# Gaps in SBUF that put the operands of TensorE at multiples of 512 bytes, in a Fourier transform with a bilinear expert

## The chip, the core and the metric

The kernel runs on one core of one Trainium2 chip. The metric is the device time of one execution in microseconds (us). TensorE (PE) does the matrix products, VectorE (DVE), ScalarE (ACT) and GpSimd (POOL) the elementwise work, and SyncE (SP) and POOL issue the DMAs. SBUF is the memory that holds the engines' operands; a byte address in this text is one within a partition, and every tile has the same address in all of its 128 partitions. PSUM takes TensorE's results.

## The reference

```python
X = np.fft.fft(x, axis=1)             # x: 8 x 3072 x 256, float32
X = np.fft.fft(X, axis=2).real
X = X.reshape(8 * 3072, 256)
a = X @ w_a                           # 256 x 1536
b = X @ w_b                           # 256 x 1536
out = (a * b) @ w_out                 # 1536 x 256
```

## The kernel before

The transform along the 256 features is folded into the weights: `w_a` and `w_b` are multiplied once, at the start, by a cosine and a sine matrix (`WChunk`, L497, plain float32), and the result stands in SBUF in two tiles, `W0` and `W1`. The transform along the 3072 positions is done for each of the 8 batches by matmuls of the folded input with tables of cosines and sines: `dft_mm` (L179) and `dft_quad` (L191), whose moving operand is a table `tab` and whose stationary operand (weights, in TensorE's sense) is `XH`, the folded input. The results are the rows of `PQ`: 1536 frequencies wide, a cosine part and a sine part.

A number is kept as a sum of a high and a low part of type float32r, and each product is made in three passes, high by high, high by low and low by high (`PASSES`). So each table holds a high and a low row for each of three blocks: `tab` is `[P, 3, 2, TW]`, with `TW` numbers of 4 bytes in a row. The first 386 of them at most are read.

The main work is 288 units: 8 batches `b`, 3 blocks `st` of 512 frequencies, 12 blocks `ft` of 128 of the 1536 hidden features. A unit has 24 matmuls with 512 columns each:

- `mm_e` (L759), 6 matmuls: the cosine part of `PQ` is the moving operand, 128 columns of `W0` or `W1` are the weights. The result is `ab`, one PSUM bank for `a` and one for `b`.
- `mm_o` (L773), 6 matmuls: the same with the sine part of `PQ`, added to `ab`.
- `mm_d` (L851), 12 matmuls: the product `a * b` (its high part `gh` and its low part `gl`) is the moving operand, every second column of a row of `WO` (a step of 8 bytes, 128 columns) the weights. The result is `d`, held for the 12 `ft` of a block.

```python
nc.tensor.matmul(ab[i], wcols(lh, 0, i, ft * P, P), PQ[:, rh, st * 512 : (st + 1) * 512], ...)   # L759
nc.tensor.matmul(cur["d"][s][h], WO[:, rh, ft, h:D:2], gg[lh][:, s, :], ...)                     # L851
```

Between them DVE, ACT and POOL turn `ab` into `gh` and `gl`. In the last block of the last batch `mm_rows` (L726) takes `gh` and `gl` as weights and 256 columns of `WO` as the moving operand, and `ExUp` and `ExDown` (L958, L962, L987, L990) do 48 matmuls with very few weight columns for two single frequencies.

The order of the work is written out by hand in the list `units` and by the function that walks through it. Tiles come from pools. A pool's tiles lie behind each other in the order of their first request, each rounded up to 32 bytes, and the pools lie behind each other in the order in which they were made. A pool with two buffers (`tb` for the tables, `t`, `bc`, `g`) repeats its tiles. `PQ` and `PN` are requested late, in the middle of the set-up, and are the last tiles of the pool `per`; `tb` is the pool behind it, and `t`, `bc`, `g` and the staging follow; the pool `late` with `W1` and `XH` is last.

Of the kernel before, what the change touches and what calls it, by code (L numbers as in the profile page):

```python
# [7 lines left out]
F32 = mybir.dt.float32  # L8
# [3 lines left out]
ALU = mybir.AluOpType  # L12
PSUM = bass.MemoryType.PSUM

TW = 386

@with_exitstack
def fft2_real__then__bilinear_moe_kernel(
# [26 lines left out]
    P = 128  # L45
# [4 lines left out]
    J = S // 8  # L50

    per = ctx.enter_context(tc.tile_pool(name="per", bufs=1))
    dram = ctx.enter_context(tc.tile_pool(name="dram", bufs=1, space=bass.MemoryType.DRAM))
    tb_p = ctx.enter_context(tc.tile_pool(name="tb", bufs=2))
    t_p = ctx.enter_context(tc.tile_pool(name="t", bufs=2))
# [3 lines left out]
    ps_ab = ctx.enter_context(tc.tile_pool(name="ps_ab", bufs=2, space=PSUM))  # L59
    ps_d = ctx.enter_context(tc.tile_pool(name="ps_d", bufs=1, space=PSUM))  # L60

    W0 = per.tile([P, 2, 2, 1024], F32R, name="W0")
    WO = per.tile([P, 2, NFT, D], F32R, name="WO")
    w128 = per.tile([P, 2 * NFT], F32, name="w128")
# [20 lines left out]
    def f32(ap):  # L85
        return ap.bitcast(F32)

    def split(lo_eng, hi, lo, src):
        nc.scalar.copy(hi, src)
        lo_eng.tensor_tensor(lo, src, f32(hi), ALU.subtract)  # L90
# [65 lines left out]
    def sign_ops(kind):  # L156
        f = F[:, kind, 0:5:4, :]
        nc.scalar.activation(f, f, AF.Copy, scale=sm[:, 0:1])
        f = F[:, kind, 2, :]
        nc.scalar.activation(f, f, AF.Copy, scale=sm[:, 1:2])  # L160
# [9 lines left out]
    def load_tab(half, q):  # L170
        t = tb_p.tile([P, 3, 2, TW], F32R, tag="tab", name="tab")
        nc.gpsimd.dma_start(t.rearrange("p a b c -> p (a b c)"), tabs[3 * half + q])
        tabq[(half, q)] = t
# [10 lines left out]
    def dft_quad(ps, lhs, r, tab, swap):  # L184

        own, e, o = r
        for rr, kt, c0, c1 in ((own, own // 2, 0, TW), (o, 0, 0, J // 2), (e, 0, J // 2, TW)):
            if kt == 0 and swap:
                rr = e + o - rr
            for k, (lh, rh) in enumerate(PASSES):  # L190
                nc.tensor.matmul(  # L191
                    ps[:, c0:c1], lhs(lh, rr), tab[:, kt, rh, c0:c1],
                    start=(c1 - c0 == TW and k == 0), stop=(c1 == TW and kt == 0 and k == 2), skip_group_check=True,
                )

    def dft_pair4(q, ps=None):
        ps = ps or ab_tiles()

        def lhs(h, r):
            return XH[:, h, q, r, :]  # L200

        dft_quad(ps[0], lhs, (5, 1, 3), tabq[(0, 2 * q)], q == 1)
        dft_quad(ps[1], lhs, (2, 0, 4), tabq[(0, 1)], q == 1)
        return ps
# [20 lines left out]
    def dft_pair32(kind, half, q, ps, f=None):  # L225

        f = f or (lambda r: F[:, kind, r, :])
        for i, (t, n) in enumerate(((q, halves(half)[2] if q == 0 else J), (1, J))):
            for kt in range(3):
                nc.tensor.matmul(  # L230
                    ps[i][:, 0:n], f(2 * kt + 1 - i), tab32[(half, t)][kt][:, 0:n], start=(kt == 0), stop=(kt == 2)
                )
# [15 lines left out]

    def halves(half):
        cols = slice(2 * J * half, 2 * J * (half + 1))  # L250
        return cols, (J + 1 if half == 0 else J), (TW if half == 0 else J)

    def pairs2(v):
        return v.rearrange("p (i t) -> p i t", t=2)
# [1 line left out]
    def combine(dst, a, ps, m, quad=False):  # L256

        lo, hi, av, cv = dst[:, 0:J], dst[:, J : 2 * J][:, ::-1], a[0:m, 0:J], ps[1][0:m, 0:J]
        if quad:
            lo, hi, av, cv = pairs2(lo), pairs2(hi), pairs2(av), natural(ps[1][0:m], J // 2)  # L260
        nc.vector.tensor_tensor(lo, av, cv, ALU.add)
        nc.vector.tensor_tensor(hi, av, cv, ALU.subtract)
# [9 lines left out]
    class DftP:  # L272
# [4 lines left out]
        def mm(self, ps=None):  # L277
            if self.b == 0:
                self.ps = ps
                return dft_pair32(2 * self.half, self.half, 0, ps)  # L280
            if self.quad:
                self.ps = dft_pair4(0, ps)
                return
            self.ps = dft_pair(
                lambda h, kt: XH[:, h, 0, 2 * kt + 1, :], lambda h, kt: XH[:, h, 0, 2 * kt, :],
                self.half, 0, halves(self.half)[2], ps,
            )

        def copy(self):
            b, half, ps = self.b, self.half, self.ps  # L290
            n0 = halves(half)[1]
            a = self.a = bc_p.tile([P, 512], F32, tag="bc", name="bc")
            evened(a, ps[0], n0, self.quad, zb[:, half, b : b + 1])

        def sums(self):
            b, half, ps, a = self.b, self.half, self.ps, self.a
            self.t = t_p.tile([P, 1024], F32, tag="T", name="T")[:, 0 : 2 * J]
            combine(self.t, a, ps, P, self.quad)
            nc.scalar.copy(PQ[:, 0, halves(half)[0]], self.t)

# [5 lines left out]
        def low(self, lo_eng=nc.gpsimd):  # L306
            cols = halves(self.half)[0]
            lo_eng.tensor_tensor(PQ[:, 1, cols], self.t, f32(PQ[:, 0, cols]), ALU.subtract)

# [64 lines left out]
    class DftQ:  # L374
# [53 lines left out]
        def split(self, lo_eng=nc.gpsimd):  # L428
            cols, _, _ = halves(self.half)

            nc.scalar.copy(self.t[0:1, :], PN[0:1, cols])
            split(lo_eng, PQ[:, 2, cols], PQ[:, 3, cols], self.t)

# [49 lines left out]
    def wcols(h, eo, i, c, n):  # L483

        return W0[:, h, eo, 512 * i + c : 512 * i + c + n] if c < 512 else W1[:, h, eo, 1024 * i + c - 512 : 1024 * i + c - 512 + n]

# [33 lines left out]
    class WHalf:  # L520
# [12 lines left out]
        def dst(self, lh, eo):  # L533
            return W0[:, lh, eo, :].rearrange("p (i c) -> p i c", i=2)[:, :, 256 * self.h : 256 * (self.h + 1)]

# [83 lines left out]
    for half in range(2):  # L619
        t = tb_p.tile([P, 3, 2, TW], F32, tag="tab", name="tab32").rearrange("p a b c -> p (a b c)")  # L620
        for q in range(3):
            v = t[:, 3 * TW * q : 3 * TW * (q + 1)] if q < 2 else room.tile([P, 3 * TW], F32, name=f"tab32_{half}")
            nc.sync.dma_start(v, tabs32[3 * half + q])
# [29 lines left out]
    p0.copy()  # L653
    sign_ops(1)
    q0.mm()
    PQ = per.tile([P, 4, H], F32R, name="PQ")
    PN = per.tile([P, H], F32, name="PN")
    p0.sums()
# [94 lines left out]
    def mm_e(u):  # L753
# [3 lines left out]
        for i in range(2):  # L757
            for k, (lh, rh) in enumerate(PASSES):
                nc.tensor.matmul(  # L759
                    ab[i], wcols(lh, 0, i, ft * P, P), PQ[:, rh, st * 512 : (st + 1) * 512],  # L760
                    start=(k == 0), stop=(k == 2), skip_group_check=True,
# [7 lines left out]
    def mm_o(u, ab):  # L769
        b, st, ft = u  # L770
        for i in range(2):
            for k, (lh, rh) in enumerate(PASSES):
                nc.tensor.matmul(  # L773
                    ab[i], wcols(lh, 1, i, ft * P, P), PQ[:, 2 + rh, st * 512 : (st + 1) * 512],
                    start=False, stop=(k == 2), skip_group_check=True,
# [472 lines left out]
def tables(S, D):  # L1248
    import numpy as np

    def hi_lo(c):
        def r12(v):
            u = np.ascontiguousarray(v.astype(np.float32)).view(np.uint32)
            u = (u + np.uint32(0x7FF) + ((u >> np.uint32(12)) & np.uint32(1))) & np.uint32(0xFFFFF000)
            return u.view(np.float32)

        hi = r12(c)
        return hi, r12(c - hi.astype(np.float64))

    H, J = S // 2, S // 8  # L1260
    p = np.arange(128)[:, None, None]
    kt = np.arange(3)[None, :, None]
    j = np.arange(J + 1)[None, None, :]
    tabs = np.zeros((6, 128, 3, 2, TW), np.float32)
    for half in range(2):
        s = 2 * j + half
        for q in range(3):
            n = 6 * p + 2 * kt + (1 if q == 1 else 2)
            ang = 2.0 * np.pi * ((s * n) % S) / S
            v = np.sin(ang) if q == 2 else np.cos(ang)  # L1270
            if (half, q) in ((0, 0), (1, 2)):
                v = v * np.where(n == S // 4, 0.5, 1.0)
            tabs[3 * half + q, :, :, 0, : J + 1], tabs[3 * half + q, :, :, 1, : J + 1] = hi_lo(v)
    wtab = np.zeros((128, 2, 2, 128), np.float32)
    d = 2 * np.arange(128)[:, None, None] + np.arange(2)[None, :, None]
    m = np.arange(128)[None, None, :]
    ang = 2.0 * np.pi * ((d * m) % D) / D
    co = np.cos(ang)
    si = -np.sin(ang)
    si[:, :, 0] = (1 - 2 * (d % 2))[:, :, 0]  # L1280
    for eo, v in enumerate((co, si)):
        wtab[:, :, eo] = v
    tabs32 = tabs.sum(axis=3, dtype=np.float64).astype(np.float32)
    tabs[:3] = tabs[:3][..., np.r_[1:J:2, 0 : J + 1 : 2, J + 1]]
    small = np.zeros((128, 20), np.float32)
    small[:, 0] = 1 - 2 * (np.arange(128) % 2)
    small[:, 1] = -small[:, 0]
    small[:, 2] = -1.0
    small[0, 2] = 1.0
    small[:16, 4:20] = np.eye(16)  # L1290
    return {
        "tabs": tabs.reshape(6, 128, -1),
        "small": small,
        "mirror": np.ascontiguousarray(np.eye(128, dtype=np.float32)[::-1]),
        "tabs32": tabs32.reshape(6, 128, -1),
        "wtab32": wtab.reshape(128, -1),
    }
# [29 lines left out]
```

## Time and profile before

| | us |
|---|---|
| three runs, median (lowest to highest) | 1777.65 (1777.24 to 1778.70) |
| the profiled execution, its own time | 1777.32 |
| span of its instructions | 1775.6 |
| PE busy | 1754.3 (99% of the span), 7774 matmuls |
| PEld (weight loads, beside the matmuls) busy | 1437.2 (81%) |
| DVE busy | 1380.7 (78%) |
| POOL busy | 1104.6 (62%) |
| ACT busy | 651.3 (37%) |

A matmul's record runs from its start to the modelled end of its last column, and the next one starts before that. The duration in a record (some 394 ns) is therefore not what a matmul costs. What it costs is the distance from its start to the start of the next one, which the text calls its pitch; it is read from the start times in the timeline.

### The profile page before, as it was taken

The numbers are of one execution on the slowest core, as the hardware profiler recorded it, in microseconds if no ns is written. First come the engines' busy times: TensorE is split into PE (matmuls) and PEld (weight loads), VectorE is DVE, ScalarE is ACT, GpSimd is POOL, SyncE is SP. The second block draws the span as 40 slices with busy tenths as digits, with TensorE's granted clock in tenths as the row PEclk, the third lists the DMA queues.
The fourth block names the chain that finished last, engine by engine and source line by source line (L and its number), as shares of the span: only waits on it lengthen the run. The fifth ranks groups of instructions, "written<-read, shape, count | busy, mean of one in ns | idle before, by whom it ended". The sixth has DMA issues, their size and how long they took to land.

```text
span 1775.6 us, 22491 instructions
## 1 busy us (share of the span) xinstructions
PE 1754.3 (99%) x7774; PEld 1437.2 (81%) x7774; DVE 1380.7 (78%) x2128; ACT 651.3 (37%) x1165; POOL 1104.6 (62%) x894
## 2 busy tenths in 40 slices
PE   7999999999999999999999999999999999999999
PEld 4677778888888888888888888888888888888788
DVE  7878977787788776887777887778778787677766
ACT  4653343333433334333343334333343333333333
POOL 1577766666666665666666666666667666544443
PEclk9999999999999999999999999999999999999999
DMA  6223343211222122410233102321123121210130
GB/s 250 100 92 52 78 147 117 72 48 46 94 82 76 38 48 99 128 40 26 66 110 105 48 10 75 104 99 48 40 85 95 66 48 46 89 51 18 10 27 25
DMA packets 179521, 128.69 MB, mean 72 GB/s; under 512 B 154574, under 2 KB 157550, under 8 KB 173518
## 3 DMA queue, kind: packets, MB, share of 16 engines
q1 hardware_dynamic: 168414, 61.97, 14.3%
q0 software_dynamic: 10448, 64.23, 10.9%
q8 instruction: 61, 1.00, 0.2%
q10 hardware_dynamic: 544, 1.05, 0.2%
q14 instruction: 54, 0.44, 0.1%
HBM read 97.95 MB, written 29.25 MB: 72 GB/s over the span
## 4 chain that ended last, share of the span: by engine, by line
PE 94%; DVE 3%; ACT 1%; issue 1%; DMA 0%; POOL 0%; DVEq 0%; ACTq 0%; POOLq 0%
PE d L851 42%; PE ab L759 22%; PE ab L773 22%; PE ab L179 3%; PE ab L191 2%; PE d L726 2%; PE ab L497 1%; DVE T L763 1%; PE d L230 0%; DVE T L789 0%; DMA RAW<-in_x_dram,rix 0%; DVE F L458 0%; PE ab L531 0%; DVE g L779 0%; DVE F L457 0%
## 5 line engine op out<-in xcount | busy, mean ns | idle before, releaser
L809 POOL TENSOR_TENSOR gl<-g,gh 128x512 fp32r<-128x512 f32 x574 | 759.1, 1343 | 527.8 <-ACT gh L780 525.6
L789 DVE SCALAR_TENSOR_TENSOR T<-T,ab 128x512 f32<-128x512 f32 x576 | 369.2, 682 | 327.2 <-PE ab L773 326.0
L851 PE MATMUL d<-gh,WO 128*128 128x512 f32 x2208 | 612.2, 394 | 0.0
L851 PEld LDWEIGHTS d<-gh,WO 128*128 128x128 f32 x2208 | 427.4, 194 | 87.9 <-DVE WO L461 0.4
L759 PE MATMUL ab<-PQ,W 128*128 128x512 f32 x1728 | 452.0, 397 | 1.5 <-DVE g L779 1.1
L773 PE MATMUL ab<-PQ,W 128*128 128x512 f32 x1728 | 447.5, 394 | 3.6 <-DVE T L763 3.6
L763 DVE SCALAR_TENSOR_TENSOR T<-PN,w,ab 128x512 f32<-128x512 f32 x576 | 404.6, 742 | 31.7 <-PE ab L759 24.9
L759 PEld LDWEIGHTS ab<-PQ,W 128*128 128x128 f32 x1728 | 324.1, 188 | 78.9 <-DVE g L779 2.6
L773 PEld LDWEIGHTS ab<-PQ,W 128*128 128x128 f32 x1728 | 323.3, 188 | 79.7 <-DVE T L763 4.9
L780 ACT CAST gh<-g 128x512 fp32r<-128x512 f32 x288 | 178.9, 621 | 516.5 <-DVE g L779 458.6
L851 PE MATMUL d<-gl,WO 128*128 128x512 f32 x1104 | 354.9, 395 | 0.1
L792 ACT COPY bc<-ab 128x512 f32<-128x512 f32 x288 | 169.0, 587 | 500.0 <-DVE T L789 499.7
L851 PEld LDWEIGHTS d<-gl,WO 128*128 128x128 f32 x1104 | 213.2, 193 | 45.0 <-POOL gl L809 0.8
L801 DVE TENSOR_TENSOR g<-T 128x512 f32<-128x512 f32 x273 | 207.7, 761 | 0.1
L779 DVE TENSOR_TENSOR g<-ab,bc 128x512 f32<-128x512 f32 x288 | 197.2, 685 | 10.3 <-ACT bc L792 8.5
L802 ACT CAST gh<-g 128x512 fp32r<-128x512 f32 x288 | 178.5, 620 | 20.3 <-DVE g L801 19.3
L801 POOL TENSOR_TENSOR g<-T 128x512 f32<-128x512 f32 x15 | 19.3, 1284 | 62.9 <-DVE T L789 42.1
L867 DVE STREAM_TRANSPOSE stg<-d 128x512 f32<-128x512 f32 x92 | 57.6, 684 | 0.0
L90 POOL TENSOR_TENSOR XH<-F,XH 128x768 fp32r<-128x768 f32 x28 | 54.5, 1956 | 0.0
L102 POOL DMA_INDIRECT RAW<-in_x_dram,rix x44 | 44.1, 1002 | 10.5 <-issue 8.4
L179 PE MATMUL ab<-tab,XH 128*128 128x384 f32 x252 | 46.7, 338 | 0.0
L179 PEld LDWEIGHTS ab<-tab,XH 128*128 128x128 f32 x252 | 44.7, 188 | 1.2
(179 smaller groups left out, 923.0 us busy)
## 6 DMA issues: line engine op xcount, KB each, us to landing
tab<-in_tabs_dram POOLq DMA_DIRECT2D x42, 1158.0 KB, 5.7
RAW<-in_x_dram SPq DMA_DIRECT2D x44, 256.0 KB
out_dram<-stg SPq DMA_DIRECT2D x160, 64.0 KB
out_dram<-stg SPq DMA_DIRECT2D x58, 128.0 KB
PN<-nrow SPq DMA_DIRECT2D x14, 384.0 KB
tab<-in_tabs_dram SPq DMA_DIRECT2D x6, 579.0 KB
out_dram<-stg SPq DMA_DIRECT2D x96, 32.0 KB
RAW<-in_moe_w_a_dram SPq DMA_DIRECT2D x2, 1024.0 KB
```

The source lines that it names most:

```text
L179: nc.tensor.matmul(ps, lhs(lh, kt), tab[:, kt, rh, 0:n], start=(k == 0), stop=(k == 8))
L759: nc.tensor.matmul(ab[i], wcols(lh, 0, i, ft * P, P), PQ[:, rh, st * 512 : (st + 1) * 512], start=(k == 0), stop=(k == 2), skip_group_chec ...
L763: nc.vector.scalar_tensor_tensor(t[:, i, :], PN[:, st * 512 : (st + 1) * 512], w128[:, i * NFT + ft : i * NFT + ft + 1], ab[i], ALU.mult, ...
L773: nc.tensor.matmul(ab[i], wcols(lh, 1, i, ft * P, P), PQ[:, 2 + rh, st * 512 : (st + 1) * 512], start=False, stop=(k == 2), skip_group_che ...
L779: nc.vector.tensor_tensor(v["g"][:, 0, :], v["ab"][0], v["bc"], ALU.mult)
L780: nc.scalar.copy(v["gh"][:, 0, :], v["g"][:, 0, :])
L789: nc.vector.scalar_tensor_tensor(t[:, i, :], t[:, i, :], 2.0, ab[i], ALU.mult, ALU.subtract)
L792: nc.scalar.copy(bc, ab[1])
L801: (nc.gpsimd if v["early"] else nc.vector).tensor_tensor(g[:, 1, ::-1], t[:, 0, :], t[:, 1, :], ALU.mult)
L802: nc.scalar.copy(gh[:, 1, :], g[:, 1, :])
L809: eng.tensor_tensor(gl[:, s, :], g[:, s, :], f32(gh[:, s, :]), ALU.subtract)
L851: nc.tensor.matmul(cur["d"][s][h], WO[:, rh, ft, h:D:2], gg[lh][:, s, :], start=(ft == first and k == 0 and not seeded), stop=(ft == last ...
```

## The change

The change makes three tiles that nothing writes or reads, of 384, 128 and twice 128 bytes, and makes a table row 400 numbers long (1600 bytes, where it had 1544). The new 14 numbers of each row are zeros in the tables in memory; they are loaded and not read. Everything that meant "386 columns" by `TW` now says `J + 2`, with `J` = 384, and the first and last flags of `dft_quad` are written so that they come out as before.

```diff
-TW = 386
+TW = 400
@@ pools
+    per.tile([P, 96], F32, name="gap0")
+    t_p.tile([P, 32], F32, tag="gap", name="gap2")
     W0 = per.tile([P, 2, 2, 1024], F32R, name="W0")
@@ dft_quad
-        for rr, kt, c0, c1 in ((own, own // 2, 0, TW), (o, 0, 0, J // 2), (e, 0, J // 2, TW)):
+        for rr, kt, c0, c1 in ((own, own // 2, 0, J + 2), (o, 0, 0, J // 2), (e, 0, J // 2, J + 2)):
...
-                    start=(c1 - c0 == TW and k == 0), stop=(c1 == TW and kt == 0 and k == 2), skip_group_check=True,
+                    start=(rr == own and k == 0), stop=(rr in (e, o) and c0 > 0 and k == 2), skip_group_check=True,
@@ halves
-        return cols, (J + 1 if half == 0 else J), (TW if half == 0 else J)
+        return cols, (J + 1 if half == 0 else J), (J + 2 if half == 0 else J)
@@ before PQ
+    per.tile([P, 32], F32, name="gap1")
     PQ = per.tile([P, 4, H], F32R, name="PQ")
@@ tables
-    tabs[:3] = tabs[:3][..., np.r_[1:J:2, 0 : J + 1 : 2, J + 1]]
+    tabs[:3, ..., : J + 2] = tabs[:3][..., np.r_[1:J:2, 0 : J + 1 : 2, J + 1]]
```

The addresses at which the tiles lie, from their sizes and the order of their requests:

| tile | read by PE as | bytes | address before, past a multiple of 512 | address now, past a multiple of 512 |
|---|---|---|---|---|
| `W0` | weights, L759 and L773 | 16384 | 16512, 128 | 16896, 0 |
| `WO` | weights, L851; moving, L726 | 24576 | 32896, 128 | 33280, 0 |
| `PQ` | moving, L759 and L773 | 24576 | 87552, 0 | 88064, 0 |
| `tab`, first buffer | moving, L179 and L191 | 9264, now 9600 | 118272, 0 | 118784, 0 |
| `tab`, second buffer | moving, L179 and L191 | 9264, now 9600 | 127552, 64 | 128384, 384 |
| `gh`, two buffers | moving, L851; weights, L726 | 4096 each | 157312 and 161408, 128 | 158720 and 162816, 0 |
| `gl`, two buffers | moving, L851; weights, L726 | 4096 each | 165504 and 169600, 128 | 166912 and 171008, 0 |
| `W1` | weights, L759 and L773 | 32768 | 181888, 128 | 183296, 0 |
| `XH` | weights, L179 and L191 | 12288 | 214656, 128 | 216064, 0 |

All slices of `W0`, `W1`, `WO`, `PQ`, `gh`, `gl` and `XH` that a 512-column or transform matmul starts at lie at multiples of 512 bytes within their tile (in `WO` also 4 bytes past one). Rows of `tab` start every 1544 bytes before, so at multiples of 8 bytes, and every 1600 bytes now, at multiples of 64. `T`, `bc`, `g` and the staging move by the same amounts as `gh`; PSUM is not touched.

The order of the instructions is the same on every engine, row for row, and so is what each waits for. Only addresses differ, and the size of the table loads.

## Rows read from the trace of the kernel before

**Rows 1.** The page: busy time, share of the span and instructions by engine; granted clock.
```profile
PE 1754.3 (99%) x7774; PEld 1437.2 (81%) x7774; DVE 1380.7 (78%) x2128; ACT 651.3 (37%) x1165; POOL 1104.6 (62%) x894
...
PEclk9999999999999999999999999999999999999999
```
**Rows 2.** The page: chain that ended last, shares of the span by engine and line.
```profile
PE 94%; DVE 3%; ACT 1%; issue 1%; DMA 0%; POOL 0%; DVEq 0%; ACTq 0%; POOLq 0%
PE d L851 42%; PE ab L759 22%; PE ab L773 22%; PE ab L179 3%; PE ab L191 2%; PE d L726 2%; PE ab L497 1%; DVE T L763 1%; PE d L230 0%; DVE T L789 0%; DMA RAW<-in_x_dram,rix 0%; DVE F L458 0%; PE ab L531 0%; DVE g L779 0%; DVE F L457 0%
```
**Rows 3.** What PE waited for: us in total, times, longest.
```profile
PE pz L603 <- DVE zr L600: 6.0, 1, 6.0
PE ab L531 <- DVE u L459: 5.2, 1, 5.2
PE ab L773 <- DVE T L763: 3.6, 4, 1.7
PE ab L759 <- DVE g L779: 1.1, 2, 0.8
```
**Rows 4.** Matmuls by line and form, costliest first.
```profile
L851 PE MATMUL d<-gh,WO 128*128 128x512 f32 x2208 | 612.2, 394 | 0.0
L759 PE MATMUL ab<-PQ,W 128*128 128x512 f32 x1728 | 452.0, 397 | 1.5 <-DVE g L779 1.1 <-DVE tabw L1029 0.3
L773 PE MATMUL ab<-PQ,W 128*128 128x512 f32 x1728 | 447.5, 394 | 3.6 <-DVE T L763 3.6
L851 PE MATMUL d<-gl,WO 128*128 128x512 f32 x1104 | 354.9, 395 | 0.1
```
**Rows 5.** Timeline of PE, one unit: start us, us, what, count.
```profile
799.67 1.55 PE L773 MATMUL ab<-PQ,W 128*128 128x512 f32 x6
801.06 1.56 PE L759 MATMUL ab<-PQ,W 128*128 128x512 f32 x6
802.45 1.09 PE L851 MATMUL d<-gh,WO 128*128 128x512 f32 x4
...
805.25 1.55 PE L773 MATMUL ab<-PQ,W 128*128 128x512 f32 x6
```
**Rows 6.** Timeline of PE, eight matmuls of `ExUp`: W moving, 48 or 16 weight columns.
```profile
1644.54 0.40 PE L958 MATMUL ab<-W,XH 128*48 128x512 f32 x1
...
1646.15 0.39 PE L962 MATMUL ab<-W,XH 128*16 128x512 f32 x1
1646.38 0.86 PE L851 MATMUL d<-gh,WO 128*128 128x512 f32 x3
```
**Rows 7.** Timeline of PE, plain float32 matmuls of the set-up, two records for each.
```profile
18.75 4.05 PE L230 MATMUL d<-tab,F 128*128 128x386 f32 x12
22.64 4.04 PE L230 MATMUL d<-tab,FN 128*128 128x386 f32 x12
```
**Rows 8.** Weight loads by line and form: busy us, mean ns.
```profile
L851 PEld LDWEIGHTS d<-gh,WO 128*128 128x128 f32 x2208 | 427.4, 194 | 87.9 <-DVE WO L461 0.4
L759 PEld LDWEIGHTS ab<-PQ,W 128*128 128x128 f32 x1728 | 324.1, 188 | 78.9 <-DVE g L779 2.6 <-issue 1.2 <-DVE tabw L1029 0.5
```
**Rows 9.** Timeline of PE, a transform of 18 matmuls and what follows.
```profile
705.38 3.33 PE L179 MATMUL ab<-tab,XH 128*128 128x384 f32 x18
708.55 1.56 PE L759 MATMUL ab<-PQ,W 128*128 128x512 f32 x6
709.95 0.63 PE L851 MATMUL d<-gh,WO 128*128 128x512 f32 x2
```
**Rows 10.** Matmuls with the tables, by line and form.
```profile
L179 PE MATMUL ab<-tab,XH 128*128 128x384 f32 x252 | 46.7, 338 | 0.0
L191 PE MATMUL ab<-tab,XH 128*128 128x386 f32 x84 | 19.9, 345 | 0.0
L191 PE MATMUL ab<-tab,XH 128*128 128x194 f32 x84 | 14.0, 276 | 0.0
L191 PE MATMUL ab<-tab,XH 128*128 128x192 f32 x84 | 13.4, 267 | 0.0
```
**Rows 11.** DMA issues of the page: count, KB each, median us from issue to landing.
```profile
tab<-in_tabs_dram POOLq DMA_DIRECT2D x42, 1158.0 KB, 5.7
tab<-in_tabs_dram SPq DMA_DIRECT2D x6, 579.0 KB
```

## The prediction

> **What bounds the kernel now.** I read the page's busy shares first, then the chain, the waits of PE, and then the timeline for start times. PE is busy for 99% of the span at the full granted clock, the upper of its two levels, 2.4 GHz [rows 1]. The chain of the work that ended last is 94% PE, and 86% of the span are three lines, L851, L759 and L773 [rows 2]. PE's waits are few: two of 5 to 6 us in the set-up and a handful below 2 us, all on DVE and none on a DMA [rows 3]. So DVE, ACT, POOL and the queues are covered, and the time is the number of matmuls times their pitch, and little else.
>
> The three lines hold 1728 + 1728 = 3456 matmuls with `PQ` moving and 2208 + 1104 = 3312 with `gh` or `gl` moving [rows 4], 6768 in all, each of 512 columns. Their pitch in a unit [rows 5]: six of L773 take 801.06 - 799.67 = 1.39 us and six of L759 take 802.45 - 801.06 = 1.39 us, 231.7 ns each; twelve of L851 take 805.25 - 802.45 = 2.80 us, 233.3 ns each. At 2.4 GHz with one column per cycle 512 columns would take 213.3 ns. So each matmul loses 18.3 ns (`PQ`) or 20.0 ns (`gh`, `gl`), and all together 3456 x 18.3 + 3312 x 20.0 = 129 us, 7% of the span. That is what the change can reach for; nothing else in the trace is that large and moves with an address.
>
> What the loss hangs on shows in three places. Plain float32 matmuls, which take a column only every second cycle of a record, hardly have it: twelve records with 385 columns on average take 22.64 - 18.75 = 3.89 us [rows 7], 324 ns each, against 385 x 2 / 2.4 = 320.8 ns, so 3.4 ns are lost. The loss belongs to reading four bytes per cycle. Second, with hardly any weights to load it shrinks only a little: the eight `ExUp` matmuls, 48 or 16 weight columns, take 1646.38 - 1644.54 = 1.84 us [rows 6], 230.0 ns each. So it is mostly the moving stream, and the weight stream adds 1.7 to 3.3 ns. Third, addresses: in L851 both operands lie 128 bytes past a multiple of 512; in L759 and L773 only the weights do. L851 is the slower one by 1.7 ns. Its weights also have a step of 8 bytes, and their loads are longer, 194 ns against 188 [rows 8], so the 1.7 ns have two possible causes.
>
> **The change part by part.** No instruction is added, taken away or moved on any engine or queue; only addresses differ. So the sum is made of pitches.
>
> *L851*: `gh`, `gl` and `WO` come to 0. The nearest row is that of `PQ`, a moving operand at 0 already, 231.7 ns. I take it that L851 gets there: 3312 x 1.67 ns = -5.5 us. Bounds: nothing, if the 1.67 ns are the weights' step; and 230.0 ns [rows 6], 3312 x 3.33 = -11.0 us.
>
> *L759 and L773*: `PQ` stays at 0, `W0` and `W1` come to 0. No row shows full weights at 0 beside a float32r stream at 0. From below, the change can't do better by the weights than to take them away almost altogether, 230.0 ns [rows 6]: 3456 x 1.67 = -5.8 us. From above, moving operand and weights then share one offset, as they do in L851 now, 233.3 ns: +5.8 us. I take half of the gain, 0.83 ns, since the weights are still read, if with a straight start: -2.9 us.
>
> *Transforms*: 504 matmuls have `tab` moving and `XH` as weights [rows 10]. Eighteen take 708.55 - 705.38 = 3.17 us [rows 9], 176.1 ns each, where 384 columns need 160.0. `XH` comes to 0, table rows from multiples of 8 bytes to multiples of 64, the second buffer of `tab` from 64 to 384 past 512 (so not every operand is brought to 512). I put it at 0. If an eighth of the 16.1 ns moved either way, it would be 504 x 2.0 = 1.0 us.
>
> *Table loads*: 42 loads of 1158 KB grow by 14/386 = 3.6% to 1200 KB, and 5.7 us to landing [rows 11] by at most 0.2 us each. PE waits for no DMA [rows 3], so nothing; without that cover it would be 42 x 0.2 = 8.6 us. The six loads at the start grow by 21 KB each; PE waits there for DVE [rows 3].
>
> *The others*: DVE, ACT and POOL do the same work; even if an elementwise operation changed with its address, they are off the chain [rows 2].
>
> Sum: -5.5 - 2.9 = -8.4 us. The profiled execution's own time, 1777.3 us, becomes 1768.9; the median of the runs stands 0.3 above it, so **1769.2 us**. Of the whole loss of 129 us that is a fifteenth.
>
> **The rivals.**
>
> *It changes nothing.* The moving operand of `ExUp` is `W0` or `W1`, 128 past 512, and its pitch of 230.0 ns is below that of `PQ`, which starts at 0 [rows 5, 6]. So 128 bytes need not cost a moving stream anything, and the 1.67 ns of L851 may be its weights' step [rows 8]. Then the time stays at 1777.6 us. Against it stands only that L851 and `PQ` differ. The Trainium skill, "SBUF — State Buffer", in the note on cachelines under "Door 1: The DMA port swizzle", says that SBUF is read in lines of 16 bytes, at full bandwidth where a line is hit at least twice. All operands of the three lines are at multiples of 16 bytes now, so by that rule the gaps are worth nothing. The trace agrees with it so far as `ExUp` goes; but a contiguous stream should by it lose nothing at all, and here it loses 18 to 20 ns.
>
> *The loss is paid at each crossing of a multiple of 512 bytes.* A moving row of 2048 bytes crosses four of them when it starts at 128, and three when it starts at 0; weights of 512 bytes cross one, then none. L851 would go from four to three in its stream, a quarter of 20.0 ns: 3312 x 5.0 = -16.6 us. L759 and L773 go from three and one to three: 3456 x 4.6 = -15.8 us. Together -32.4 us, 1745.3 us. For it: the loss grows with the length of the row (16.1 ns at 384 columns, 20.0 at 512). Against it: `PQ` with its three crossings and `ExUp` with four are not in that order.
>
> *Slower: operands with the same offset hinder each other.* The line that has both operands at one offset from 512 is the slow one today, L851 [rows 5]. The change gives L759 and L773 the same state. If the two read ports meet where their addresses are equal modulo some size, L759 and L773 rise to 233.3 ns, 3456 x 1.67 = +5.8 us, and L851, whose offsets stay equal, gains nothing: 1783.4 us. This wins if L851 gains less than 1.7 ns. Six L759 matmuls just after a transform already take 709.95 - 708.55 = 1.40 us [rows 9], 233.3 ns, so the state exists for these operands.
>
> *The loss goes away.* With the pitch at 213.3 ns and the 3.4 ns that float32 keeps [rows 7], 216.7 ns: 3456 x 15.0 + 3312 x 16.6 = 107 us less, 1671 us. `PQ`, half aligned, shows nothing of this, so it is unlikely. The Trainium skill, "TensorE: Matmul & The Clock Gate", in the section on the 2.5 ns, gives 215.7 ns for back-to-back matmuls of 512 columns at the full clock, in bf16; by it the gain would be some 114 us (an estimate). The trace disagrees with it for float32r.
>
> **How the numbers follow.** Within 0.2% (3.6 us) a measurement of this kernel can't tell a difference from none. Chances: the forecast's gain 0.35, its own range 1760.8 us (all three lines at 230.0 ns, -16.8 us) to 1774.0; crossings 0.17; the loss gone 0.03; no change 0.26; slower 0.19. So faster 0.55, same 0.26, slower 0.19. The range leaves out the vanished loss and the tails: from the rival of crossings, 1745.3, with 1 us for the transforms, 1744, to the slower rival with 1 us for the transforms and 1.5 of the table loads' 8.6, 1786.
>
> **What would show it.** In the timeline of the changed kernel a unit takes 5.55 us in place of 5.58, with twelve L851 matmuls in 2.78 and six of L759 or L773 in 1.385. Crossings: a unit near 5.46, L851 at 228. Slower: L759 and L773 at 1.40 for six. No change: the same start distances to 10 ns. PE should stay above 98% busy at the full clock, and its waits should not name a DMA. The prediction is wrong in its ground if the pitch changes nowhere and the time still moves, or if the pitch moves by more than 5 ns: then the offset from 512 does more than the difference between L851 and L759 shows.

## The result, and the profile after

The changed kernel takes 1763.66 us (median; 1763.39 to 1764.09), the kernel before 1777.84 in the same comparison: a ratio of 0.992, with a 95% interval of 0.9903 to 0.9937. That is 14 us or 0.8% faster, in the range of the prediction and in its direction, and 5.5 us below its 1769.2 us.

The page's busy time and chain of the changed kernel (their lines are numbered two or three higher: L762 is `mm_e`, L776 `mm_o`, L854 `mm_d`):

```profile
PE 1740.6 (99%) x7774; PEld 1435.1 (81%) x7774; DVE 1382.5 (78%) x2128; ACT 651.8 (37%) x1165; POOL 1107.9 (63%) x894
...
PE 93%; DVE 4%; ACT 1%; issue 1%; POOL 0%; DMA 0%; DVEq 0%; SPq 0%; ACTq 0%
```

PE bounds the kernel as before [rows 1, 2]; its busy time fell by 13.7 us, as much as the span, which went from 1775.6 to 1762.0. The groups of matmuls by line and form say where:

```profile
L854 PE MATMUL d<-gh,WO 128*128 128x512 f32 x2208 | 612.4, 394 | 0.0
L762 PE MATMUL ab<-PQ,W 128*128 128x512 f32 x1728 | 444.0, 392 | 1.5 <-DVE g L782 1.1 <-DVE tabw L1032 0.3
L776 PE MATMUL ab<-PQ,W 128*128 128x512 f32 x1728 | 441.2, 391 | 3.5 <-DVE T L766 3.5
L854 PE MATMUL d<-gl,WO 128*128 128x512 f32 x1104 | 354.9, 394 | 0.1
```

Against [rows 4], `mm_e` fell from 452.0 to 444.0 us and `mm_o` from 447.5 to 441.2, 14.3 us together. `mm_d` stands where it stood: 612.2 and 612.4, 354.9 and 354.9. So the whole gain is in the matmuls with `PQ` moving. One unit in the timeline (start us, us, what, count), which answers to [rows 5]:

```profile
799.99 1.53 PE L776 MATMUL ab<-PQ,W 128*128 128x512 f32 x6
801.35 1.52 PE L762 MATMUL ab<-PQ,W 128*128 128x512 f32 x6
802.72 1.09 PE L854 MATMUL d<-gh,WO 128*128 128x512 f32 x4
...
805.52 1.53 PE L776 MATMUL ab<-PQ,W 128*128 128x512 f32 x6
```

Twelve matmuls with `PQ` take 802.72 - 799.99 = 2.73 us, 227.5 ns each, where they took 2.78, 231.7 ns. Twelve of `mm_d` take 805.52 - 802.72 = 2.80 us, 233.3 ns, as before. A unit went from 5.58 to 5.53 us; 288 units times 0.05 are the 14 us. The transforms did not move: 18 matmuls still take 704.11 - 700.95 = 3.16 us (3.17 in [rows 9]).

```profile
700.95 3.33 PE L181 MATMUL ab<-tab,XH 128*128 128x384 f32 x18
704.11 1.54 PE L762 MATMUL ab<-PQ,W 128*128 128x512 f32 x6
705.50 0.63 PE L854 MATMUL d<-gh,WO 128*128 128x512 f32 x2
```

The six of `mm_e` right behind a transform still take 705.50 - 704.11 = 1.39 us, though their operands lie as in the unit above, where six take 1.37.

`ExUp`, whose pitch of 230.0 ns [rows 6] had served as a bound, became slower: its eight matmuls take 1633.83 - 1631.96 = 1.87 us, 233.8 ns.

```profile
1631.96 0.40 PE L961 MATMUL ab<-W,XH 128*48 128x512 f32 x1
...
1633.83 1.09 PE L854 MATMUL d<-gh,WO 128*128 128x512 f32 x4
```

### The profile page after: what moved, and what is told of

It reads as the page before. It is cut to its first block, busy times and chain, and to the rows that moved or that the text cites. A ratio compares the mean times of both kernels' runs of the same rounds, so it can differ in the third digit from the quotient of the medians.

```text
span 1762.0 us, 22491 instructions
## 1 busy us (share of the span) xinstructions
PE 1740.6 (99%) x7774; PEld 1435.1 (81%) x7774; DVE 1382.5 (78%) x2128; ACT 651.8 (37%) x1165; POOL 1107.9 (63%) x894
## 4 chain that ended last, share of the span: by engine, by line
PE 93%; DVE 4%; ACT 1%; issue 1%; POOL 0%; DMA 0%; DVEq 0%; SPq 0%; ACTq 0%
PE d L854 43%; PE ab L776 22%; PE ab L762 22%; PE ab L181 3%; PE ab L193 2%; PE d L729 2%; PE ab L499 1%; DVE T L766 1%; DVE F L460 0%; DVE T L792 0%; DVE F L459 0%; DVE g L782 0%; DMA zr<-in_x_dram 0%; ACT bc L795 0%; POOL gl L812 0%
## 5 line engine op out<-in xcount | busy, mean ns | idle before, releaser
L854 PE MATMUL d<-gh,WO 128*128 128x512 f32 x2208 | 612.4, 394 | 0.0
L854 PEld LDWEIGHTS d<-gh,WO 128*128 128x128 f32 x2208 | 426.8, 193 | 87.8 <-DVE WO L463 0.4
L762 PE MATMUL ab<-PQ,W 128*128 128x512 f32 x1728 | 444.0, 392 | 1.5 <-DVE g L782 1.1
L776 PE MATMUL ab<-PQ,W 128*128 128x512 f32 x1728 | 441.2, 391 | 3.5 <-DVE T L766 3.5
L776 PEld LDWEIGHTS ab<-PQ,W 128*128 128x128 f32 x1728 | 323.3, 188 | 76.3 <-DVE T L766 5.1
L762 PEld LDWEIGHTS ab<-PQ,W 128*128 128x128 f32 x1728 | 322.8, 188 | 70.8 <-DVE g L782 2.8
L854 PE MATMUL d<-gl,WO 128*128 128x512 f32 x1104 | 354.9, 394 | 0.1
L854 PEld LDWEIGHTS d<-gl,WO 128*128 128x128 f32 x1104 | 213.2, 193 | 45.0 <-POOL gl L812 0.8
```

Of the source, the lines that this page charges most:

```text
L776: nc.tensor.matmul(ab[i], wcols(lh, 1, i, ft * P, P), PQ[:, 2 + rh, st * 512 : (st + 1) * 512], start=False, stop=(k == 2), skip_group_che ...
```

## The experiments

All of them change addresses by gaps, or the order in which numbers stand in a tile. "Start" is the place of an operand past a multiple of 512 or 256 bytes; two operands "start alike" when that place is the same.

**Which operand did it?** Three kernels. `w_only` starts from the kernel before and moves the weights `W0` and `W1` alone:

```diff
+    per.tile([P, 96], F32, name="gapa")
     W0 = per.tile([P, 2, 2, 1024], F32R, name="W0")
+    per.tile([P, 160], F32, name="gapb")
...
+    late.tile([P, 96], F32, name="gapc")
     W1 = late.tile([P, 2, 2, 2048], F32R, name="W1")
+    late.tile([P, 32], F32, name="gapd")
```

> The kernel before with gaps that move W0 and W1 alone to multiples of 512 (from 128 past one); every other operand of PE keeps its offset from a multiple of 1024. Theory A (the start of the weights decides): six matmuls of mm_e or mm_o take 1.36 us as in the changed kernel, twelve of L851 still 2.80, a unit 5.53, time 1764 us, the whole gain. Theory B (moving operand and weights with the same offset are good): the same here, since PQ is at 0. Theory C (PQ gains because it moved from 512 past a multiple of 1024 to 0): a unit stays at 5.58, 1777.7 us.

Measured: 1771.3 us, ratio 0.9968 (0.9953 to 0.9982); 6 us, less than half of the gain.

```profile
802.49 1.55 PE L775 MATMUL ab<-PQ,W 128*128 128x512 f32 x6
803.88 1.54 PE L761 MATMUL ab<-PQ,W 128*128 128x512 f32 x6
805.26 1.08 PE L853 MATMUL d<-gh,WO 128*128 128x512 f32 x4
...
808.05 1.55 PE L775 MATMUL ab<-PQ,W 128*128 128x512 f32 x6
```

Six of `mm_o` take 1.39, six of `mm_e` 1.38, twelve of `mm_d` 2.79. No theory had this: the weights of `mm_e` and `mm_o` start as their moving operand does and the pitch is still 230 to 232 ns. What the trace shows of it stands with the borders between groups, below. The second kernel, `w_off`, takes the changed kernel and puts `W0` and `W1` back to 128:

```diff
-    per.tile([P, 96], F32, name="gap0")
     t_p.tile([P, 32], F32, tag="gap", name="gap2")
     W0 = per.tile([P, 2, 2, 1024], F32R, name="W0")
+    per.tile([P, 96], F32, name="gapb")
...
+    late.tile([P, 32], F32, name="gapc")
     W1 = late.tile([P, 2, 2, 2048], F32R, name="W1")
+    late.tile([P, 96], F32, name="gapd")
```

> The changed kernel with W0 and W1 put back to 128 past a multiple of 512; all other operands stay where the change put them. Theories A and B: a unit goes back to 5.58 us and the time to 1777.7 us. Theory C: a unit stays at 5.53, 1763.7 us. If gh, gl and WO at 0 helped by the state that they leave behind for the next matmuls, something between.

Measured in one run: 1779.9 us, with a unit of 806.53 - 800.94 = 5.59 us.

```profile
800.94 1.56 PE L776 MATMUL ab<-PQ,W 128*128 128x512 f32 x6
802.34 1.56 PE L762 MATMUL ab<-PQ,W 128*128 128x512 f32 x6
...
806.53 1.56 PE L776 MATMUL ab<-PQ,W 128*128 128x512 f32 x6
```

Theory C falls: without the weights at 0 the change is worth nothing, or worse. The third, `same128`, moves only `PQ` and `PN` of the kernel before, to the start that all the other operands of the units have there:

```diff
+    per.tile([P, 32], F32, name="gapa")
     PQ = per.tile([P, 4, H], F32R, name="PQ")
     PN = per.tile([P, H], F32, name="PN")
+    per.tile([P, 96], F32, name="gapb")
```

> The kernel before with PQ (and PN) moved to 128 past a multiple of 512, where W0 and W1 are already, so that both operands of mm_e and mm_o have one offset, which is not 0. Theory A: a unit stays at 5.58 us or gets longer, since the weights start at 128 as before; 1777 us or more. Theory B: a unit 5.53, 1764 us. The rival of the prediction by which operands with one offset hinder each other: six of mm_e or mm_o take 1.40, 1783 us.

Measured in one run: 1763.71 us.

```profile
799.91 1.53 PE L775 MATMUL ab<-PQ,W 128*128 128x512 f32 x6
801.28 1.52 PE L761 MATMUL ab<-PQ,W 128*128 128x512 f32 x6
802.64 1.09 PE L853 MATMUL d<-gh,WO 128*128 128x512 f32 x4
...
805.44 1.53 PE L775 MATMUL ab<-PQ,W 128*128 128x512 f32 x6
```

This is the changed kernel's unit, 5.53 us, with no operand at a multiple of 512 but the first table. So it is not the multiple of 512 that counts but that the operands start alike. `PQ` was the odd one out in the kernel before. Theory A and the prediction's slower rival fall here; theory B stands, with `w_only` left to explain.

**What holds `mm_d` at 233.3 ns?** `wo_flat` stores the even columns of `WO` ahead of the odd ones, so that the weights of `mm_d` are 512 contiguous bytes:

```diff
-                lambda e: nc.scalar.copy(hi, u),
+                lambda e: nc.scalar.copy(hi, u.rearrange("p (t m h) -> p t m h", t=4, h=2)),
...
-        return [WO[:, h, 4 * q : 4 * q + 4, :].rearrange("p a b -> p (a b)") for h in range(2)]
+        return [WO[:, h, 4 * q : 4 * q + 4, :].rearrange("p t (h m) -> p t m h", h=2) for h in range(2)]
...
-                    cur["d"][s][h], WO[:, rh, ft, h:D:2], gg[lh][:, s, :],
+                    cur["d"][s][h], WO[:, rh, ft, P * h : P * (h + 1)], gg[lh][:, s, :],
```

The low part is written in the same way, and the copies behind `mm_rows` and `ExDown` turn the columns back.

> The changed kernel with the columns of WO stored with the even ones first and the odd ones behind them, so that the weights of L851 are 512 contiguous bytes in place of every second number of 1024; the few matmuls that read WO as moving operand get their columns in that order and the copies of their results turn it back. If the step of the weights is what keeps L851 at 233.3 ns while L759 and L773 went to 227: twelve of L851 take 2.72 us in place of 2.80, a unit 5.45, time 3312 x 6.4 ns less, 1742 us. If L851 is held by its moving operand (written by other engines just before): a unit stays at 5.53, 1763.7 us.

Measured: 1744.5 us, ratio 0.9813 (0.9797 to 0.9829). It is faster than both kernels.

```profile
798.31 1.52 PE L779 MATMUL ab<-PQ,W 128*128 128x512 f32 x6
799.67 1.52 PE L765 MATMUL ab<-PQ,W 128*128 128x512 f32 x6
801.03 1.07 PE L857 MATMUL d<-gh,WO 128*128 128x512 f32 x4
...
803.75 1.52 PE L779 MATMUL ab<-PQ,W 128*128 128x512 f32 x6
```

Twelve of `mm_d` take 2.72 us, 226.7 ns, and so do those of `mm_o` and `mm_e` now (six in 1.36 us): a unit is 5.44 us. The weight loads of `mm_d` also went to the 188 ns of the contiguous ones [rows 8]:

```profile
L857 PEld LDWEIGHTS d<-gh,WO 128*128 128x128 f32 x2208 | 414.5, 188 | 88.8 <-DVE WO L463 1.6 <-ACT WO L462 0.6
```

The edit changes two things at once: the step goes, and the odd columns, which started 4 bytes past the even ones, now start 512 bytes past them. No run separates the two. For the step speaks that in the changed kernel the loads of even and of odd columns last the same 193 ns, though the even ones start as `gh` and `gl` do.

**The start within how many bytes, and does each difference cost the same?** Four kernels move all weights of the units together (and `XH`, which lies behind `W1`), with the moving operands left at 0, all from `wo_flat`. Where `k` is the weights' start, the edit is

```diff
-    per.tile([P, 96], F32, name="gap0")
+    per.tile([P, 96 + k // 4], F32, name="gap0")
...
     WO = per.tile([P, 2, NFT, D], F32R, name="WO")
+    per.tile([P, 128 - k // 4], F32, name="gapb")
...
+    late.tile([P, k // 4], F32, name="gapc")
     W1 = late.tile([P, 2, 2, 2048], F32R, name="W1")
```

> The kernel of wo_flat with all weights of the units (W0, W1, WO) at 256 past a multiple of 512, all moving operands (PQ, gh, gl) at 0. Theory D (what costs is a difference between the start of the moving operand and that of the weights, modulo 512): the unit is longer than the 5.44 us of wo_flat, 5.55 to 5.6, 1770 us or more. Theory E (what costs is that the difference changes from one group of matmuls to the next): a unit of one even pitch, 5.44 or another value, no more than 5.47. Theory F (only the place within 256 bytes counts): exactly as wo_flat, 5.44 and 1744.5 us.

> The kernel of wo_flat with all weights of the units (W0, W1, WO) at 64 past a multiple of 512, all moving operands at 0. Theory D: longer than 5.44 us, 5.55 to 5.6. Theory E: one even pitch, a unit of 5.44 or little else. If only the place within 64 bytes counts: exactly as wo_flat, 1744.5 us.

Measured: 1743.77 us at 256 and 1784.46 at 64, one run each. At 256, six of `mm_e` take 1.36 us and twelve of `mm_d` 2.72, as in `wo_flat`:

```profile
798.81 1.52 PE L766 MATMUL ab<-PQ,W 128*128 128x512 f32 x6
800.17 1.07 PE L858 MATMUL d<-gh,WO 128*128 128x512 f32 x4
...
802.89 1.52 PE L780 MATMUL ab<-PQ,W 128*128 128x512 f32 x6
```

At 64, six take 1.40 and twelve 2.80, 233.3 ns on average; the starts of the single matmuls in the trace alternate between some 231 and 236 ns:

```profile
799.22 1.56 PE L766 MATMUL ab<-PQ,W 128*128 128x512 f32 x6
800.62 1.09 PE L858 MATMUL d<-gh,WO 128*128 128x512 f32 x4
...
803.42 1.56 PE L780 MATMUL ab<-PQ,W 128*128 128x512 f32 x6
```

So a difference costs, as in theory D, but one of 256 bytes counts as none (theory F): it counts modulo 256 and not 512. A difference that is the same in all groups is no help, and theory E falls.

> The kernel of wo_flat with all weights at 192 past a multiple of 512, the moving operands at 0. By fw64 (233.3 ns) and fw256 (226.7 ns): 233.3 ns if any difference modulo 256 costs the same, a unit 5.60, 1784 us. If the place within 256 bytes sets how much is lost, another pitch between 220 and 233.

> The kernel of wo_flat with all weights at 32 past a multiple of 512, the moving operands at 0. If any difference modulo 256 costs the same: 233.3 ns, a unit 5.60, 1784 us. If only the place in steps of 64 bytes counts: 226.7 ns, 5.44, 1744 us. A pitch below 226.7 would beat all kernels so far.

Measured, one run each: 1783.75 us at 32, with the unit of 5.60 us of 64 (here from one `mm_o` to the next):

```profile
802.95 1.56 PE L780 MATMUL ab<-PQ,W 128*128 128x512 f32 x6
...
808.55 1.56 PE L780 MATMUL ab<-PQ,W 128*128 128x512 f32 x6
```

And 1756.65 at 192, with another pitch:

```profile
799.87 1.54 PE L766 MATMUL ab<-PQ,W 128*128 128x512 f32 x6
801.24 1.08 PE L858 MATMUL d<-gh,WO 128*128 128x512 f32 x4
...
803.99 1.54 PE L780 MATMUL ab<-PQ,W 128*128 128x512 f32 x6
```

Six take 1.37 us, 228.3 ns, and twelve 2.75, 229.2. The place within 256 bytes thus sets how much is lost: nothing more than the least at 0, 6.6 ns more at 32 and 64, some 2 at 192 (which is 64 below a multiple of 256). None is below 226.7.

**Does a change of start from one group to the next cost?** `fgh128` moves `gh` and `gl` alone, `fgroup` moves `gh`, `gl` and `WO` together, both to 128 and from `wo_flat`; `wo_flat_b` gives the kernel before the new order of `WO` and no gaps.

```diff
+    ga_p = ctx.enter_context(tc.tile_pool(name="ga", bufs=1))
     g_p = ctx.enter_context(tc.tile_pool(name="g", bufs=2))
...
+    ga_p.tile([P, 32], F32, name="gapx")
...
+    per.tile([P, 32], F32, name="gapa")
     WO = per.tile([P, 2, NFT, D], F32R, name="WO")
+    per.tile([P, 96], F32, name="gapb")
...
+    late.tile([P, 32], F32, name="gapc")
     W1 = late.tile([P, 2, 2, 2048], F32R, name="W1")
```

That is `fgroup`, in which `W1` comes to 256, as good as 0 by `fw256`; `fgh128` has the first gap alone, with 384 bytes behind the pool.

> The kernel of wo_flat with gh and gl alone moved to 128 past a multiple of 512; PQ and all weights stay at 0. Theory D: L851 is slowed to 232 to 234 ns, L759 and L773 stay near 227, a unit 5.51 to 5.53, some 1765 us. Theory E: both groups are disturbed, as in w_only, a unit 5.5 to 5.57. If a moving operand written just before is not what counts and the offset neither: 5.44.

> The kernel before, no gaps, with the columns of WO in the order of wo_flat. gh, gl and WO all lie at 128 there, PQ at 0 with its weights at 128. Theory D: L851 goes to 227 ns, L759 and L773 stay at 231.7: a unit 5.50, 1777.4 - 3312 x 6.5 = 1756 us. Theory E: L851 stays disturbed by the groups beside it, a unit 5.53 to 5.58, 1765 to 1777 us.

> The kernel of wo_flat with PQ, W0 and W1 at multiples of 256 and gh, gl and WO all at 128 past a multiple of 512: within each group of matmuls the moving operand and the weights start alike, from group to group the start changes. Theory D alone (a difference within a matmul, modulo 256): 226.7 ns everywhere but at the first one or two matmuls of a group, a unit 5.44 to 5.46, 1744 to 1750 us. If the change from group to group costs as well (the reading of w_only): a unit 5.48 to 5.56, 1757 to 1772 us.

Measured, one run each: 1767.94, 1767.12 and 1750.39 us. In `fgh128`, `mm_e` keeps 1.36 us and `mm_d` goes to 802.77 - 799.98 = 2.79:

```profile
798.62 1.52 PE L769 MATMUL ab<-PQ,W 128*128 128x512 f32 x6
799.98 1.09 PE L861 MATMUL d<-gh,WO 128*128 128x512 f32 x4
...
802.77 1.54 PE L783 MATMUL ab<-PQ,W 128*128 128x512 f32 x6
804.14 1.52 PE L769 MATMUL ab<-PQ,W 128*128 128x512 f32 x6
```

In `wo_flat_b` it is the other way round. `mm_o` and `mm_e`, whose operands differ by 128, take 1.39 and 1.40 us; the first six of `mm_d`, whose operands both start at 128, take 1.38 and the next six 807.34 - 805.98 = 1.36:

```profile
801.81 1.55 PE L776 MATMUL ab<-PQ,W 128*128 128x512 f32 x6
803.20 1.56 PE L762 MATMUL ab<-PQ,W 128*128 128x512 f32 x6
804.60 1.08 PE L854 MATMUL d<-gh,WO 128*128 128x512 f32 x4
...
805.98 1.07 PE L854 MATMUL d<-gh,WO 128*128 128x512 f32 x4
...
807.34 1.55 PE L776 MATMUL ab<-PQ,W 128*128 128x512 f32 x6
```

Which group is slow is as theory D has it, in both. The time of `wo_flat_b` is not: with a unit of 5.53 us and 1767.12 us it lies where theory E was put, 11 us above the 1756 of theory D. What theory D lacks is an after-effect. In the start times of the single matmuls (median of 237 units of each trace), the first three matmuls behind a group with unlike starts are slow too, though their own operands start alike: 232, 232, 231 and then 227 ns at the head of `mm_d` in `wo_flat_b` and at the head of `mm_o` in `fgh128`.

In `fgroup`, where all groups have like starts, a unit takes 805.94 - 800.48 = 5.46 us, 0.02 more than in `wo_flat`; 288 times 0.02 are the 6 us by which it is slower. A change of start from group to group costs, but little: it is paid at the border, by the last and the first matmul of a group (231 to 233 ns), and the others keep 227.

```profile
800.48 1.53 PE L783 MATMUL ab<-PQ,W 128*128 128x512 f32 x6
801.85 1.53 PE L769 MATMUL ab<-PQ,W 128*128 128x512 f32 x6
803.21 1.07 PE L861 MATMUL d<-gh,WO 128*128 128x512 f32 x4
...
805.94 1.53 PE L783 MATMUL ab<-PQ,W 128*128 128x512 f32 x6
```

`w_only` has the same change of start between its groups, with the stepped weights in `mm_d`, and there the after-effect reaches through nearly all of `mm_o` and `mm_e`: 228, 235, 233, 236, 224, 231 and 236, 228, 233, 231, 227, 228 ns. It does settle, at the eleventh of these twelve. In the last block, where `mm_rows` stands in the place of `mm_d`, it settles sooner: six of `mm_o` still take 1.39 us, but six of `mm_e` take 1706.93 - 1705.57 = 1.36, as in `wo_flat`.

```profile
1704.18 1.55 PE L775 MATMUL ab<-PQ,W 128*128 128x512 f32 x6
1705.57 1.53 PE L761 MATMUL ab<-PQ,W 128*128 128x512 f32 x6
1706.93 0.40 PE L728 MATMUL d<-WO,gh 128*128 128x256 f32 x2
```

So like starts give 226.7 ns in `w_only` too, where what ran before has died away; that is how its 6 us and theory B go together. Why the after-effect lasts three matmuls in one kernel and ten in another was not tried.

**The table rows.** `row386` is the changed kernel with `TW = 386` again, and 896 bytes behind the tables that keep everything else in place.

> The changed kernel with table rows of 386 numbers again; one gap behind the tables keeps every operand but the second buffer of the tables (64 past a multiple of 512) where the change put it. If the rows of the tables matter: eighteen transform matmuls change by more than 0.05 us and the time by more than 1 us. If, as the two traces say, all of the gain is in L759 and L773: 1763.7 us, transforms within 0.4 us in total.

Measured in one run: 1764.56 us, with the unit of 5.53 us. The longer rows and their loads are worth nothing that one run can show.

## Why the prediction was right, and where not

The ground was right: the time is the number of matmuls times their pitch, the change acts on the pitch alone, DVE, ACT, POOL and the queues stay covered, and the table loads and the transforms cost nothing. The cause was not. The prediction went by each operand's own place past a multiple of 512; what counts is the place of the weights relative to that of the moving operand, and `same128`, which moves `PQ` away from 0, has the whole gain. That the time came out in the range, 14.2 us lower against a sum of 8.4, is therefore in part luck: the larger term of the sum was nothing, and the smaller one was five times too small.

*"I take it that L851 gets there", -5.5 us*: measured 0, the bound that the prediction gave "if the 1.67 ns are the weights' step". The operands of `mm_d` started alike already (but for the odd columns of `WO`, 4 bytes further) and do so still. What set it apart from `PQ` was the step, or the 4 bytes that come with it: `wo_flat` takes both away and `mm_d` falls from 233.3 to 226.7 ns.

*L759 and L773, -2.9 us*: measured -14.3 in busy time, 4.2 ns a matmul, where the bounds of the prediction were 1.67 ns either way. The bound from below, "the change can't do better by the weights than to take them away almost altogether, 230.0 ns", was the error that mattered. The eight `ExUp` matmuls were read as a stream without weights. Their weights lie at the start of `XH`, at 128 past a multiple of 256 before and at 0 now, as `W0` and `W1` do: they start like the moving operand in both kernels, and take 230.0 and 233.8 ns, while the full matmuls went to 227.5. So they don't follow the rule of the full ones and bound nothing for them; why, no run shows. By the same reading "the weight stream adds 1.7 to 3.3 ns" was too little: `fw64` and `wo_flat` differ in where the weights start, and by 6.6 ns. The prediction's sign that more is at work, a pitch that moves by more than 5 ns, was not reached by the change (4.2 ns) and was by that experiment.

*The rivals.* That operands with one start hinder each other is the reverse of what the runs show; [rows 5] could not tell it, since L851 differs from the others in the step as well. The 1.40 us of six L759 matmuls just behind a transform [rows 9], which the prediction took as that state, hangs on what ran before and not on their own starts alone: in the changed kernel, with one start for all of them, six take 1.39 us behind a transform and 1.37 behind `mm_o`. Crossings of 512 fall with `same128`, which has as many as the kernel before or more, and is as fast as the changed one. "It changes nothing" falls with the ratio. The Trainium skill's note on cachelines ("SBUF — State Buffer", "Door 1: The DMA port swizzle") spoke for it: all starts but those of the odd columns of `WO` were multiples of 16 bytes. Here a difference of 32 bytes between two operands costs 6.6 ns of each matmul, so the measurement decides against that use of the note. The Trainium skill, "TensorE: Matmul & The Clock Gate", in "What happens when you issue a matmul", says that weights are loaded through a read port of their own and take no bandwidth from the running matmul. The runs do not bear that out for float32r: `wo_flat` and `fw64` differ in where the weights start relative to the moving operand, and the pitch of the matmuls goes from 226.7 to 233.3 ns with it.

*What stays open*: why the difference counts modulo 256, how the after-effect comes about, and the 226.7 - 213.3 = 13.4 ns, 91 us over 6768 matmuls, that even equal starts leave. No run went below 226.7 over a unit.

## What to carry to other kernels

Where PE is the bound with float32r, read its pitch from the start times and compare it with the columns over the clock: what is left over can be a matter of addresses, and it repeats from unit to unit (in the changed kernel nine of ten units have the same length to 5 ns). Let the weights be contiguous, and let weights and moving operand start at the same place modulo 256 bytes, and keep that place the same from group to group: its change alone cost `fgroup` 6 us. A pool's small tiles shift everything behind them, so the start is worth a look after each change of a tile's size. A multiple of 512 for its own sake is not needed.

## What was not expected of the hardware

- The pitch of a 512-column float32r matmul with 128 weight columns depends on the difference between the starts of its operands: 226.7 ns at 0 and 256 bytes, 233.3 at 32 and 64, 231.7 (the kernel before) to 233.3 (`mm_e` of `wo_flat_b`) at 128, 228.3 to 229.2 at 192.
- A group with unlike starts slows the group behind it: the first three matmuls in `wo_flat_b` and `fgh128`. Behind stepped weights that start elsewhere it was ten, in `w_only`.
- Weights with a step of 8 bytes cost 233.3 ns beside a moving operand that starts like their even columns, and their loads last 193 ns in place of 188; the 4 bytes by which the odd columns start later were not tried alone.
- A matmul with 16 or 48 weight columns is hardly faster than one with 128, or slower: 230.0 ns beside 231.7 in the kernel before, 233.8 beside 227.5 in the changed one, though its operands start alike in both.
